# Expert 0's first two weight splits and two small copies on VectorE, and four loads in another order ahead of the constants

## The chip, the cores and the metric

The kernel runs on one core of a Trainium2 chip. The metric is device time in microseconds (us) of one execution; lower is better. The time before is the median of three runs. The profile and its trace are of one more execution, taken by the hardware profiler, and all times of instructions below are counted from the start of that execution's span.

## The reference

Three layers follow each other. The first is a gated linear attention (an mLSTM) over 768 steps for 2 batches of 8 heads of width 40; its output becomes 1536 rows of 320. The second is a mixture of 8 experts with a noisy router that picks two per row. The third is a dense layer with h·cos(h) between two products.

```python
for t in range(S):                                  # attention
    m_new = np.maximum(f_gate[:, :, t] + m, i_gate[:, :, t])
    f_stab = np.exp(f_gate[:, :, t] + m - m_new)
    i_stab = np.exp(i_gate[:, :, t] - m_new)
    C = f_stab[:, :, None, None] * C + i_stab[:, :, None, None] * np.einsum('bhd,bhe->bhde', vt, kt)
    n = f_stab[:, :, None] * n + i_stab[:, :, None] * kt
    y[:, :, t] = sigmoid(o_gate) * (C @ q) / np.maximum(np.abs(n @ q), 1.0)
...
noisy_logits = x @ w_gate + np.log1p(np.exp(x @ w_noise)) * noise        # experts
top2 = np.argpartition(-noisy_logits, 2, axis=1)[:, :2]
out[mask] += top2_w[mask, k, None] * (np.maximum(x[mask] @ w1[e], 0.0) @ w2[e])
...
h = x @ w_in; return (h * np.cos(h)) @ w_out                              # dense layer
```

## The kernel before, in words

**Attention.** The 768 steps of each batch are cut into 6 chunks of 128, so there are 12 chunks, numbered 0 to 11; chunk n is one call of `att_step(n)`. The gates of all chunks lie in one small tile (`g_all`, 16 rows); VectorE scans them in pieces (`gates_a`, chunks 0, 1, 2 to 3, 4 to 5). From chunk 2 on, the scanned gates are written to memory (`gd`, line 102) and read back spread over 128 partitions (`gb`, `load_gb`, line 175). `load_qk(n)` (lines 167, 168) fetches queries and keys into one of three buffers, `load_kv` and `load_o` the values and output gates. All of these go through the queue of SyncE (SP), which issues in the order of the program; an issue that waits holds everything behind it. `late_consts` (lines 370 to 372) fetches three constants over the same queue: `cc` (masks and ramps), `wc` (router weights) and `nz` (router noise). At the end of chunk 0 VectorE makes the mask `tri` from `cc` (line 891), ahead of its state update (line 293) and the scans of chunks 4 and 5 (line 90).

In a chunk, ScalarE makes the decay weights from `gb` (`mk_w`, line 209), GpSimd masks them (line 210), VectorE multiplies them into the scores (`mk_p`, line 256), TensorE makes scores (`mm_s`, line 247), outputs (`mm_out`, lines 306 and 310) and the state (`mm_state`, line 266, which reads `kb`, made by GpSimd at line 229). `mk_decay` (line 277) decays the state on GpSimd, `mk_q` (line 237) scales the queries on GpSimd or VectorE. `mk_y` makes the output rows `xt` on VectorE (line 327), a small copy of 64 columns follows (line 329, GpSimd in every chunk), and SP writes the rows to memory (`xd`, line 330). `rt_a` turns them on TensorE (line 342), `rt_b` multiplies by the router weights (line 351).

**Experts.** Beside chunks 8 to 11, batch 0 is routed: `router_d` on VectorE ends in the row numbers `idxe` (line 511), GpSimd gathers rows by them (`gather`, line 542, tile `xgt`), and `prep_slot` turns the gathered rows on TensorE (line 551). Weights come in by `load_w` over SP (`wraw`, line 528). `split(k)` takes piece k of them apart into two parts: ScalarE copies one (`wh`, line 580), and a subtraction makes the rest (`wl`, line 582), on GpSimd or VectorE by the rule at line 581. `expert_step` multiplies (`mm1` at line 589, `mm2` at lines 594 to 598). Experts 0 and 1 have first a group for batch 0 alone, which begins during chunk 10; split 0 is asked for after chunk 8 and split 1 after chunk 9. After chunk 11 the six other experts run, then the dense layer (`moe2_step`).

**Order.** Nothing reorders the program: each engine runs its instructions in the order in which the Python code emits them (`at`, `pre`, `mid` and `fill` say after which chunk a step is emitted), and semaphores keep the engines apart. Each DMA of SP also waits for the landing of the eighth DMA before it on that queue.

Of the kernel before, what the change touches and what calls it, by code (L numbers as in the profile page):

```python
# [22 lines left out]
DM = H * D  # L23
# [9 lines left out]
KW = 384  # L33
# [7 lines left out]
def tile_mlstm_moe_moe2(ctx, tc, qk, kv, og, gi, gf, wcat, noise, wm1, wm2, cst, out):  # L41
    nc = tc.nc
    V, A, G, T, Y = nc.vector, nc.scalar, nc.gpsimd, nc.tensor, nc.sync
# [79 lines left out]
    def gates_c(c0, c1):  # L123
        pv = PT[c0]
        V.tensor_copy(tok[:, c0:c1, :], pv[:, :, 0:16])
        if c0 < 2:
            V.tensor_copy(tokG[:, c0:c1, :], pv[:, :, 64:80])
        A.activation(kdec[:, c0:c1, :], pv[:, :, 32:48], AF.Exp)
# [23 lines left out]
    def load_o(i):  # L152
        t = OT[i] = mp.tile([128, 2, KO], FT, name="ogt", tag="wl" if i % 2 else "wh", bufs=4)
        Y.dma_start(t, og[:, 2 * i:2 * i + 2, :])
# [6 lines left out]
    def load_qk(n):  # L161
        if n >= 2 * NC:
            return
        b, c = divmod(n, NC)
        d = L[n]
        t = d["qk"] = QKS[n % NB]
        Y.dma_start(t[0:D, 0:3], qk[b, c, 0])
        Y.dma_start(t[64:64 + D, 1:4], qk[b, c, 1])

    def load_gb(n):  # L170
        if n >= 2 * NC:
            return
        b, c = divmod(n, NC)
        t = L[n]["gb"] = ap_.tile([128, H, C], FT, name="gb", bufs=3)
        Y.dma_start(t, bass.AP(tensor=GD.tensor, offset=GD.offset + (c * 16 + b * H) * C,
                               ap=[[0, 128], [C, H], [1, C]]))

    def load_kv(n):
        if n >= 2 * NC:
            return  # L180
        b, c = divmod(n, NC)
        d = L[n]
        t = ap_.tile([128, KO + H * (D + 1)], FT, name="kv", bufs=NB)
        Y.dma_start(t, kv[b, c])
        d["k"] = t[:, 0:KO].rearrange("p (h d) -> p h d", d=D)
        d["v"] = t[:, KO:].rearrange("p (h d) -> p h d", d=D + 1)
# [26 lines left out]
    def mk_e(n):  # L213
        if n >= 2 * NC:
            return
        b, c = divmod(n, NC)
        d = L[n]
        if c:
            e = d["ge"] = ap_.tile([128, NH, C], FT, name="get", bufs=2)
            for s in range(2):  # L220
                r = slice(64 * s, 64 * s + 64)
                if n >= 2:
                    A.activation(e[r], d["gb"][r, s:H:2, :], AF.Exp)
                else:
                    for u in range(2):
                        A.activation(e[r, 2 * u:2 * u + 2, :], d["pg"][u][r, s:4:2, :], AF.Exp)
        if c < NC - 1:
            kb = d["kb"] = KBS[n % 2]
            G.tensor_tensor(out=kb[:, :, 0:D], in0=d["k"],
                            in1=kdec[:, c, b * H:b * H + H][:, :, None].to_broadcast([128, H, D]), op=OP.mult)  # L230
# [19 lines left out]
    def mk_p(n):  # L250
        if n >= 2 * NC:
            return
        d = L[n]
        d["p"] = ap_.tile([128, H, C], FT, name="ppt", bufs=2)
        for u in range(2):
            V.tensor_tensor(out=d["p"][:, 4 * u:4 * u + 4, :],
                            in0=d["ps", u].rearrange("p (h t) -> p h t", t=C),
                            in1=d["w"][:, 4 * u:4 * u + 4, :], op=OP.mult)
# [56 lines left out]
    def mk_y(n):  # L315
        b, c = divmod(n, NC)
        d = L[n]
        pv = d["po"][:, :H * 41].rearrange("p (h e) -> p h e", e=41)
        den = ap_.tile([128, H, 1], FT, name="den", bufs=2)
        o = OT[n // 2][:, n % 2].rearrange("p (h d) -> p h d", d=D)  # L320
        A.activation(den, pv[:, :, D:D + 1], AF.Abs)
        V.tensor_scalar(den, den, 1.0, None, op0=OP.max)
        V.reciprocal(den, den)
        V.scalar_tensor_tensor(out=o, in0=o, scalar=1.0, in1=den.to_broadcast([128, H, D]),
                               op0=OP.add, op1=OP.mult)
        x = d["x"] = mp.tile([128, KW], FT, name="xt", bufs=3)
        V.scalar_tensor_tensor(out=x[:, :DM].rearrange("p (h e) -> p h e", e=D), in0=pv[:, :, 0:D], scalar=0.5,
                               in1=o, op0=OP.mult, op1=OP.mult)
        G.tensor_copy(x[:, DM:KW], x[:, 256:DM])
        Y.dma_start(XD[b * S + c * C:b * S + (c + 1) * C, :], x)  # L330


# [36 lines left out]
    def late_consts():  # L369
        Y.dma_start(cc_, cst[:, 128:469])  # L370
        Y.dma_start(wc, wcat)
        Y.dma_start(nz, noise)
# [158 lines left out]
    groups = [(e, T2, 2 * e) for e in (0, 1)]  # L531
# [36 lines left out]
        prep_x(d["xg"][i], groups[g][1][i], d["xh"], d["xl"], 128 * i, ps_)  # L568

    SP = {}  # L570
    POOL_SPLIT = (1, 7, 9, 11, 65, 67, 75)

    def split(k):
        g, f = divmod(k, 8)
        if g >= NG:
            return
        raw = WB[groups[g][0]]
        wh = mp.tile([128, FW], FR, name="wh", tag="wh", bufs=4)
        wl = mp.tile([128, FW], FR, name="wl", tag="wl", bufs=4)
        A.activation(wh, raw[:, f, :], AF.Copy)  # L580
        eng = V if len(groups[g][1]) == 2 and (k % 2 and k not in POOL_SPLIT or k in (12, 14)) else G
        eng.tensor_tensor(out=wl, in0=raw[:, f, :], in1=wh.bitcast(FT), op=OP.subtract)  # L582
        SP[k] = (wh, wl)

# [241 lines left out]
    gates_a(2, 4)  # L826
    gates_c(1, 2)
    mk_e(0)
    late_consts()
    load_gb(2)  # L830
    mk_p(0)
    mm_g(1)
    mk_w(1)
# [3 lines left out]
    gates_b(2, 4)  # L837

    def loads(n):
        load_qk(n + 3)  # L840
        if n > 2 or n == 0:
            load_gb(n + 3)
        load_kv(n + 2)
        if n < 5:
            load_o(n + 1)
        if n == 2:
            load_gb(4)
            load_gb(5)

    def att_step(n):  # L850
        if n == 0:
            loads(0)
# [27 lines left out]
        if n == 1:  # L880
            gates_a(4, NC)
        loads(n + 1)
        if n == 2 * NC - 1:
            mk_y(n)
        for f, a in fill.pop(n, []):
            f(*a)
        if n < 2 * NC - 1:
            mk_y(n)
# [36 lines left out]
    put(8, router_b1, 0, 1)  # L925
    put(8, router_s)
    put(8, split, 0)
    put(9, split, 1)
    mid[9] = [(router_c, (0,))]
    fill[9] = [(router_d, (0,)), (gather, (0, 0)), (gather, (0, 1))]  # L930
# [38 lines left out]
    for g in range(2, NG - 1):  # L969
        n = len(groups[g + 1][1])  # L970
# [21 lines left out]
    for f in range(12):  # L992
        k = 18 + (15 * f) // 4
# [36 lines left out]
    with tc.If(over > 0):  # L1030
# [9 lines left out]
        for b in range(B):  # L1040
            with tc.For_i(0, NC, 1) as it:
                x = mp.tile([128, KW], FT, name="xt", bufs=3)
# [10 lines left out]
                for e in range(E):  # L1053
                    acc = psA()
                    for f in range(8):
# [3 lines left out]
                        for k in range(3):  # L1059
                            n = 64 if k == 2 else 128  # L1060
# [98 lines left out]
```

## Time and profile before

| what | us |
|---|---|
| median of 3 runs | 523.4 (523.13 to 523.64) |
| profiled execution, its own time | 525.03 |
| its span | 523.3 |
| TensorE matmul busy | 490.2 (94%) |
| VectorE / ScalarE / GpSimd busy | 372.1 / 325.7 / 278.5 |

The span is nearly filled by TensorE, but matmuls are pipelined and a busy row of the profile also holds matmuls that run slowly, so the share alone does not say what a change is worth. What counts is where TensorE waits and for whom, and there the chain of waits helps: it goes back from the last instruction to whatever released each step. Its shares are TensorE 69%, VectorE 14%, DMA 7%, ScalarE 3%, GpSimd 2%; nearly all that is not TensorE lies in the first 135 us and around 300 to 330 us.

### The profile page before, as it was taken

How to read it: one execution, taken by the hardware profiler on the slowest of the kernel's cores; microseconds unless marked ns; L12 is line 12 of the kernel's file. 1: busy time of each engine (PE TensorE's matmuls, PEld its weight loads, DVE VectorE, ACT ScalarE, POOL GpSimd, SP SyncE). 2: the span in 40 equal slices, each digit the busy share in tenths (PEclk: the TensorE clock that was granted, in tenths of full speed). 3: DMA queues.
4: the chain of work that ended last, by engine and by line, in shares of the span. 5: the costliest groups of instructions: out<-in, count | busy, mean ns of one | idle time of the engine just before them, and what ended most of it. 6: DMA issues, size and time to landing. Idle time of an engine off the chain costs nothing.

```text
span 523.3 us, 9036 instructions
## 1 busy us (share of the span) xinstructions
PE 490.2 (94%) x3198; PEld 468.1 (89%) x3198; DVE 372.1 (71%) x791; ACT 325.7 (62%) x695; POOL 278.5 (53%) x246
## 2 busy tenths in 40 slices
PE   4799998999999999999999987999999999999994
PEld 3688887999899999999999976899999999999994
DVE  8774497678378777777775689688856665787772
ACT  3647867466465454545454655578787777777772
POOL 6445468665846867685857696274365347300000
PEclk9999999899999999999999999999999999999998
DMA  6789894695563828291929193030021003001001
GB/s 182 209 281 266 279 278 155 188 363 172 216 248 117 313 88 330 69 372 44 380 88 319 42 360 105 29 115 14 0 76 39 1 8 95 13 2 39 1 1 44
DMA packets 25909, 77.69 MB, mean 148 GB/s; under 512 B 3872, under 2 KB 11552, under 8 KB 25856
## 3 DMA queue, kind: packets, MB, share of 16 engines
q1 hardware_dynamic: 22752, 67.50, 37.2%
q0 software_dynamic: 3104, 9.54, 6.1%
q8 instruction: 27, 0.44, 0.3%
q14 instruction: 26, 0.21, 0.1%
HBM read 67.41 MB, written 9.62 MB: 147 GB/s over the span
## 4 chain that ended last, share of the span: by engine, by line
PE 69%; DVE 14%; DMA 7%; issue 4%; ACT 3%; POOL 2%; SPq 0%; DVEq 0%; POOLq 0%; ACTq 0%
PE pS L589 31%; PE pA L598 9%; PE pA L595 9%; PE pA L594 9%; DMA gb<-gd 2%; DMA xgt<-xd,idx 2%; PE pM L551 2%; PE pS L310 2%; PE pA L247 1%; PE pM L351 1%; PE pA L607 1%; PE pA L606 1%; POOL wl L582 1%; DVE xt L674 1%; DVE c_t L713 1%
## 5 line engine op out<-in xcount | busy, mean ns | idle before, releaser
L582 POOL TENSOR_TENSOR wl<-wraw,wh 128x704 fp32r<-128x704 f32 x69 | 122.9, 1787 | 59.9 <-ACT wh L580 56.3
L644 DVE SCALAR_TENSOR_TENSOR hb<-pS,hb 128x384 fp32r<-128x384 f32 (+2 forms) x128 | 45.9, 390 | 46.4 <-ACT hb L641 45.8
L580 ACT ACTIVATE wh<-wraw 128x704 fp32r<-128x704 f32 x80 | 62.8, 785 | 14.6 <-PE pA L606 8.2
L589 PE MATMUL pS<-xh,wh 128*128 128x448 f32 (+1 forms) x240 | 69.5, 344 | 0.4 <-ACT xh L553 0.4
L589 PE MATMUL pS<-xh,wl 128*128 128x448 f32 (+1 forms) x240 | 66.3, 330 | 0.9 <-POOL wl L582 0.9
L589 PE MATMUL pS<-xh,w 128*128 128x384 f32 x288 | 66.4, 339 | 0.5 <-DVE m_t L754 0.5
L594 PE MATMUL pA<-wh,hb 128*128 128x320 f32 x208 | 62.2, 309 | 0.0
L595 PE MATMUL pA<-wl,hb 128*128 128x320 f32 x208 | 62.2, 309 | 0.0
L739 ACT ACTIVATE m_t<-pS,magic 128x384 f32<-128x384 f32 x64 | 37.1, 579 | 30.4 <-PE pS L589 29.3
L641 ACT ACTIVATE hb<-pS 128x448 fp32r<-128x448 f32 (+1 forms) x80 | 37.6, 471 | 26.9 <-PE pS L589 20.0
L589 PEld LDWEIGHTS pS<-xh,w 128*128 128x128 f32 x288 | 50.0, 188 | 1.2 <-DVE m_t L754 1.1
L598 PE MATMUL pA<-wh,hb 128*128 128x320 f32 x208 | 44.3, 313 | 4.0 <-DVE hb L644 4.0
L754 DVE SCALAR_TENSOR_TENSOR m_t<-m_t,pS 128x384 f32<-128x384 f32 x64 | 35.4, 553 | 15.4 <-ACT m_t L753 15.1
L589 PEld LDWEIGHTS pS<-xh,wl 128*128 128x128 f32 x240 | 43.1, 190 | 3.3 <-POOL wl L582 1.1
L740 DVE TENSOR_SCALAR m_t<-m_t 128x384 f32<-128x384 f32 x64 | 23.3, 365 | 28.8 <-ACT m_t L739 28.6
L589 PEld LDWEIGHTS pS<-xh,wh 128*128 128x128 f32 x240 | 40.9, 190 | 1.4 <-ACT xh L553 0.6
L760 POOL TENSOR_TENSOR wl<-m_t,wh 128x384 fp32r<-128x384 f32 x25 | 25.4, 1017 | 31.0 <-ACT wh L758 21.7
L589 PE MATMUL pS<-xl,wh 128*128 128x448 f32 (+1 forms) x160 | 39.6, 329 | 0.0
L594 PEld LDWEIGHTS pA<-wh,hb 128*128 128x128 f32 x208 | 38.6, 186 | 0.6
L595 PEld LDWEIGHTS pA<-wl,hb 128*128 128x128 f32 x208 | 38.7, 186 | 0.6
L598 PEld LDWEIGHTS pA<-wh,hb 128*128 128x128 f32 x208 | 33.0, 186 | 6.0 <-DVE hb L644 5.9
L542 POOL DMA_INDIRECT xgt<-xd,idx x28 | 34.0, 1215 | 7.8 <-issue 3.4
(203 smaller groups left out, 1251.0 us busy)
## 6 DMA issues: line engine op xcount, KB each, us to landing
wraw<-wm SPq DMA_DIRECT2D x36, 704.0 KB
raw<-wm SPq DMA_DIRECT2D x16, 704.0 KB
qk<-qk SPq DMA_DIRECT2D x24, 240.0 KB
gb<-gd SPq DMA_DIRECT2D x10, 512.0 KB
kv<-kv SPq DMA_DIRECT2D x12, 324.0 KB
yd<-yt SPq DMA_DIRECT2D x22, 160.0 KB
wraw<-wm SPq DMA_DIRECT2D x8, 352.0 KB
xd<-xt SPq DMA_DIRECT2D x12, 192.0 KB
```

The lines of the kernel that those rows point to most:

```text
L542: G.indirect_dma_start(out=t[:n, :], out_offset=None, in_=XD[0:S, :] if g < 2 else XD[:, :], in_offset=bass.IndirectOffsetOnAxis(ap=(idxe ...
L580: A.activation(wh, raw[:, f, :], AF.Copy)
L582: eng.tensor_tensor(out=wl, in0=raw[:, f, :], in1=wh.bitcast(FT), op=OP.subtract)
L589: T.matmul(p[:, :n], w[:, 128 * k:128 * k + 128], x[:, m, :], start=(i == 0), stop=(i == 7))
L594: T.matmul(a[:n, :DM], hh[:, s], wh[:, KW:], start=first, stop=False)
L595: T.matmul(a[:n, :DM], hh[:, s], wl[:, KW:], start=False, stop=False)
L598: T.matmul(a[:n, :DM], hl[:, s], wh[:, KW:], start=False, stop=last)
L641: A.activation(hh[:, :n], p[:, :n], AF.Relu)
L644: V.scalar_tensor_tensor(out=hb[:, o:o + z - a], in0=p[:, a:z], scalar=0.0, in1=hh[:, a:z].bitcast(FT), op0=OP.max, op1=OP.subtract)
L739: A.activation(t, m["p"], AF.Identity, bias=magic, scale=0.5 / PI)
L754: V.scalar_tensor_tensor(out=s, in0=s, scalar=1.0, in1=m["p"], op0=OP.subtract, op1=OP.mult)
L760: eng.tensor_tensor(out=m["hl"], in0=m["t"], in1=m["hh"].bitcast(FT), op=OP.subtract)
```

## The change

There are three edits. The loads of chunk 2's gates and chunk 3's queries are emitted ahead of the three constants, and chunk 3's queries are no longer asked for in `loads(0)`. Splits 0 and 1 of expert 0 have their subtraction on VectorE in place of GpSimd. The small copy of chunks 9 and 10 is made by VectorE in place of GpSimd.

```diff
-        G.tensor_copy(x[:, DM:KW], x[:, 256:DM])
+        (V if n in (9, 10) else G).tensor_copy(x[:, DM:KW], x[:, 256:DM])
...
-    POOL_SPLIT = (1, 7, 9, 11, 65, 67, 75)
+    POOL_SPLIT = (7, 9, 11, 65, 67, 75)
...
-        eng = V if len(groups[g][1]) == 2 and (k % 2 and k not in POOL_SPLIT or k in (12, 14)) else G
+        eng = V if len(groups[g][1]) == 2 and (k % 2 and k not in POOL_SPLIT or k in (0, 12, 14)) else G
...
     mk_e(0)
+    load_gb(2)
+    load_qk(3)
     late_consts()
-    load_gb(2)
     mk_p(0)
...
     def loads(n):
-        load_qk(n + 3)
+        if n:
+            load_qk(n + 3)
```

On the queue of SP, right after the write of the scanned gates of chunks 2 and 3 (`gd`), this stands in the program (`+` now, `-` before; `gb` is chunk 2's gates where it has a sign and chunk 3's where it has none, `qk_88` chunk 3's queries):

```order
 L102 DMA gd<-g_all 16x4x128
+L175 DMA gb<-gd 128x1024
+L167 DMA qk_88<-qk 40x1536
+L168 DMA qk_88<-qk 40x1536
 L370 DMA cc<-cst 128x341
 L371 DMA wc<-wcat 128x48
 L372 DMA nz<-noise 128x96
-L175 DMA gb<-gd 128x1024
-L167 DMA qk_88<-qk 40x1536
-L168 DMA qk_88<-qk 40x1536
 L175 DMA gb<-gd 128x1024
 L184 DMA kv<-kv 128x648
```

The three loads have moved past the three constants; all else keeps its place.

On VectorE, at the end of chunk 8 and the start of chunk 9 (`r_rb` ends the router's step of chunk 8, `st_101` is the state update of chunk 9, `ppt` the scores for chunk 10):

```order
 L471 TENSOR_TENSOR r_so<-r_so,cc 128x8
 L472 TENSOR_TENSOR r_rb<-r_so,cc 128x8
+L582 TENSOR_TENSOR wl<-wraw,wh 128x704
 L293 TENSOR_TENSOR st_101<-pS,st_101 40x4x41 x2
 L256 TENSOR_TENSOR ppt<-pA,wt 128x512 x2
```

Split 0 now stands ahead of the state update, the scores and, further on, `router_d`.

On GpSimd, from the end of chunk 8 to chunk 10 (`kb_95` and `st_99` belong to chunk 10, the two gathers fetch expert 0's rows):

```order
 L210 AFFINE_SELECT wt<-wt 128x512 x2
-L582 TENSOR_TENSOR wl<-wraw,wh 128x704
 L229 TENSOR_TENSOR kb_95<-kv,kdec 128x8x40
 L277 TENSOR_TENSOR st_99<-st_101,get 40x4x41 x2
 L542 DMA xgt<-xd,idxe 128x384
 L542 DMA xgt<-xd,idxe 112x384
-L329 COPY xt<-xt 128x64
 L210 AFFINE_SELECT wt<-wt 128x512 x2
-L582 TENSOR_TENSOR wl<-wraw,wh 128x704
 L237 TENSOR_TENSOR qtt<-qk_93,get 128x512
```

Split 0 is gone from ahead of `kb` and the gathers; the copy of chunk 9 and split 1 are gone from behind them.

## Rows read from the trace of the kernel before

**Rows 1.** Chain of waits, 10 to 62 us: start, us, what
```profile
28.43 0.96 DVE g_all L96 x2
...
29.41 4.29 DMA gd<-g_all
...
33.76 5.75 DMA gb<-gd
```

**Rows 2.** Timeline of TensorE, 28 to 133 us; brackets: idle before, releaser
```profile
44.40 0.94 PE L351 MATMUL pM<-wc,xTt 128*128 128x128 f32 x6 [0.91 <-ACT xTt L344]
...
85.83 0.96 PE L266 MATMUL pS<-kv,kb 128*104 128x82 f32 x8 [1.05 <-POOL kb L229]
...
90.60 0.33 PE L342 MATMUL pM<-ident,xt 128*128 128x128 f32 x1 [0.92 <-POOL xt L329]
```

**Rows 3.** Timeline of all engines, 0 to 45 us
```profile
22.20 0.22 DVE L891 CAST tri<-cc 128x128 bf16<-128x128 f32 x1
...
24.76 0.67 PE L247 MATMUL pA<-qk 128*128 128x256 f32 x2 [2.02 <-DMA qk<-qk]
24.83 0.69 DVE L256 TENSOR_TENSOR ppt<-pA,wt 128x512 f32<-128x512 f32 x1 [0.47 <-POOL wt L210]
```

**Rows 4.** Chain of waits, 60 to 135 us
```profile
86.68 0.17 DVE idxe L511
...
87.80 0.32 POOL xgt L542
...
89.33 2.98 DMA xgt<-xd,idxe
...
94.48 2.39 PE pS L589 x16
```

**Rows 5.** Timeline of SP, 13 to 32 us
```profile
14.13 0.34 SPq L102 DMA_DIRECT2D gd<-g_all  x1
...
17.36 0.33 SPq L175 DMA_DIRECT2D gb<-gd  x1
...
18.15 0.33 SPq L168 DMA_DIRECT2D qk<-qk  x1
```

**Rows 6.** Windows: length; busy PE, PEld, DVE, ACT, POOL; granted clock; DMA share; GB/s
```profile
17.00:18.00 1.00, 0.84 (x9) 0.68 (x7) 0.24 (x2) 0.99 (x5) 0.77 (x2) 1.00 0.05 11
...
25.00:26.00 1.00, 1.00 (x9) 0.95 (x9) 1.00 (x2) 0.27 (x1) 0.00 (x0) 1.00 1.03 405
```

**Rows 7.** Timeline of GpSimd, 70 to 115 us
```profile
83.42 1.68 POOL L582 TENSOR_TENSOR wl<-wraw,wh 128x704 fp32r<-128x704 f32 x1
...
85.73 1.45 POOL L277 TENSOR_TENSOR st<-st,get 40x164 f32<-40x164 f32 x2
```

**Rows 8.** Groups by line and shape: busy us, mean ns of one, idle before
```profile
L582 DVE TENSOR_TENSOR wl<-wraw,wh 128x704 fp32r<-128x704 f32 x11 | 11.8, 1073 | 1.5 <-ACT wh L580 1.0 <-issue 0.4
...
L675 DVE COPY xt<-xt 128x64 f32<-128x64 f32 x12 | 3.7, 312 | 0.4
```

**Rows 9.** Timeline of VectorE, 70 to 115 us
```profile
88.01 0.49 DVE L327 SCALAR_TENSOR_TENSOR xt<-pS,ogt 128x320 f32<-128x320 f32 x1
...
92.29 0.42 DVE L554 TENSOR_TENSOR xl<-pA,xh 128x256 fp32r<-128x256 f32 x1 [3.71 <-ACT xh L553]
```

**Rows 10.** Timeline of SP, 76 to 112 us
```profile
90.58 0.34 SPq L330 DMA_DIRECT2D xd<-xt  x1
90.96 1.46 SPq L528 DMA_DIRECT2D wraw<-wm  x3
...
99.35 2.85 SPq L900 DMA_DIRECT2D yd<-cc  x3
```

**Rows 11.** The two gathers (tile `xgt`) of 98 to 102 us: issue to landing
```profile
DMA to landing us min/median/max: 3.6/4.6/5.6
```

**Rows 12.** Chain of waits, whole span, its beginning
```profile
1.28 1.91 DMA g_all<-gi
```

**Rows 13.** Windows of 1 us, columns as in group 6
```profile
93.00:94.00 1.00, 1.00 (x6) 1.00 (x6) 0.33 (x2) 0.45 (x1) 1.00 (x2) 0.50 0.75 200
```

## The prediction

> **What bounds the kernel now.** I read the chain of waits first, over two stretches, and then the timelines of the engines that it names. Behind 135 us TensorE follows TensorE nearly all the way, so whatever the change does must happen before that, in the attention and the start of the experts; what the chain loses there it loses for good, since TensorE has little idle time left in which to catch up.
>
> In the first stretch the chain runs through memory, not through an engine [rows 1]: VectorE ends the scans of chunks 4 and 5 at 29.39, their write `gd` takes 4.29 us to land, the read-back `gb` of chunk 4 another 5.75, so ScalarE can start on it at 39.5. TensorE stands idle 0.91 us for ScalarE at 44.40 [rows 2]. The `gd` write is small (16 rows of 256 numbers); that it takes 4.29 us says that it queues behind the loads issued before it. TensorE's largest single wait is earlier, 2.02 us at 24.76 for chunk 3's queries and keys [rows 3].
>
> In the second stretch the chain is VectorE up to the row numbers `idxe`, ready at 86.85, then GpSimd's first gather at 87.80, the second at 89.33, its landing 2.98 us later at 92.31, and only then TensorE [rows 4]. TensorE also waits 1.05 us for `kb` at 85.83 and 0.92 us for the copy of chunk 9 at 90.60 [rows 2], both for GpSimd. But these two waits lie ahead of 92.31, where TensorE stops in any case. They are idle time off the path.
>
> **The loads.** The first edit looks aimed at the wait at 24.76, and I do not see it help. The read of chunk 2's gates is issued at 17.36 [rows 5], not because three constants hold SP (three issues of some 0.34 us are 1 us of the 3.2 since 14.13) but because it reads what `gd`, issued at 14.13, has still to write. It stands ahead of chunk 3's queries before and after the change, so the queries go out by 18.15 as now, and land when they land now. Gain: 0, unless `gd` itself lands sooner (rival 2).
>
> What it costs is the constants' place. Now they move while the memory queues have nothing else: from 17 to 18 us the DMA share is down to 0.05, at 11 GB/s [rows 6]. Afterwards they go out behind the queries, into a stretch with a share of 1.03 at 405 GB/s [rows 6]. By their shapes they are 128 rows of 341, 48 and 96 numbers, 248 kB; at 405 GB/s that is 0.61 us. Everything behind them on SP's queue (chunk 3's gates, the next values, chunk 4's queries, in the end the `gd` write of 29.41) moves back by that much, because the chain's 4.29 us is a queue. Bounds: 0, if the constants fit into gaps; 1.2, at half that rate, since their rows are short. I take **+0.6** for ScalarE's start at 39.5, and so for TensorE at 44.40.
>
> There is a second cost. VectorE makes `tri` from `cc` at 22.20 [rows 3] and will have to wait for `cc`. Chunk 3's queries land at 24.76 by TensorE's release, `cc` behind them at about 25.2 (175 kB at the same rate). That stalls VectorE 3.0 us, with the state update, the scores and the scans of chunks 4 and 5 queued behind; 0.47 us of idle time on the way [rows 3] goes into it, so the scans end at 31.9 and not at 29.39. Does that add? From there the `gd` write needs 3.2 us, if I take what the earlier one needed until it released SP (14.13 to 17.36, rows 5), or 35.1; by the queue alone it lands at 33.70 + 0.6 = 34.3. The two are close, so I count the queue and put the other 0.8 in the range. The further waits on SP (each DMA waits for the eighth before it, and those land later now) delay loads that have a queue ahead of them anyway: 0, and up to 0.5 if that queue runs dry.
>
> **Split 0 on VectorE.** GpSimd gives up 1.68 us ahead of `kb` and the gathers [rows 7]; VectorE takes on one subtraction of 1.07 us mean [rows 8] ahead of `idxe`, which moves from 86.85 to 87.92. Now GpSimd is what the first gather waits for: its decay step ends at 87.18 [rows 7], and the gather starts 0.62 behind that. With the split gone GpSimd is early and VectorE late: the gather starts 0.1 to 0.6 us behind 87.92, at 88.0 to 88.5, which is 0.2 to 0.7 later than now. I take **+0.4**. The lower bound is -0.1: VectorE's steps there may run quicker once GpSimd does no split beside them. `kb` is ready 1.6 us earlier and TensorE's wait of 1.05 goes; but the next step, `mm_out` of chunk 10, needs VectorE's scores and queries, which come later by the 1.07, so TensorE waits there instead: 0.
>
> The Trainium skill (SBUF — State Buffer, section "Who interferes with whom") says that a VectorE instruction with two SBUF inputs and a GpSimd instruction that reads SBUF exclude each other for the whole instruction. Split 0 on VectorE stands beside `kb` on GpSimd, so by that rule `idxe` would slip by one more instruction of GpSimd, and the sum would be about 0.7 higher. The mean of 1.07 us in [rows 8] already holds subtractions beside a busy GpSimd, and nothing further is counted.
>
> **Split 1 and the two copies on VectorE.** 1.07 and twice 0.31 us [rows 8]; behind chunk 9's `xt` VectorE idles 3.71 us until 92.29 [rows 9], which covers 1.38; chunk 10's copy takes 0.31 ahead of a split that TensorE needs only a step later. The wait of 0.92 at 90.60 goes [rows 2]; TensorE comes to the gathered rows sooner and waits there longer: 0. But the copy also triggers something. SP writes chunk 9's rows when the copy is made: now at 90.58, with three weight loads behind from 90.96 [rows 10]. VectorE ends `xt` at 88.50 [rows 9], later 89.57; with 0.31 for the copy the write goes out at 89.9 and the loads from 90.3, 0.7 us earlier, and their data meets that of the second gather, which starts at 89.33 + 0.4 = 89.7. What such a meeting costs is shown one step later: beside the three `yd` writes issued from 99.35 [rows 10] the gathers need 3.6 and 5.6 us [rows 11], against 2.98. Bounds: 0 and +2.6. The loads come behind the gather's start here, and ahead of it there, so I take a value nearer the lower end, **+0.7**.
>
> The Trainium skill (DMA: Bandwidth & Descriptors, "Queues, rings and completion order") has each DMA engine take turns between its queues, a packet at a time. By that a gather beside one busy queue would need about twice its own transfer time; the 5.6 us of [rows 11] agree in kind. The sum stays.
>
> **Sum.** 0.6 + 0.4 + 0.7 = +1.7. The profiled execution, 525.03 with a span of 523.3, would become 526.7 with a span of 525.0. The median of 523.4 is 1.6 below that execution's own time; with the same difference, **525.1**. All lower bounds together give 523.3, all upper ones (1.2, 0.8, 0.5, 0.7, 2.6) 529.2, which I do not expect at once.
>
> **Rivals.** (1) *The bills are covered.* The constants slip through gaps of the queue, or the loads miss the gather; then one or two of the three terms stand, +0.4 to +1.0: 523.8 to 524.4. For it: the loads follow the gather's start. Against it: the `gd` write's 4.29 us, and the 5.6 us.
>
> (2) *Faster: `gd` lands sooner.* Place: SP's issue at 17.36, which waits 3.23 us for the write of 14.13 [rows 5]; a read of the gates at the program's start is back in 1.91 us [rows 12]. If the constants' transfers are what slows that write, then with them gone it lands up to 1.3 us sooner, chunk 2's gates and chunk 3's queries follow, and TensorE resumes at 23.5 in place of 24.76. Where the constants then fill the gap that this opens, the chain keeps the 1.3 at 44.40; with the gather at its -0.1 and no meeting that is -1.4: 522.0. Where they still cost their 0.6 it is -0.8: 522.6. It decides from the point where the gain at 17.36 passes the constants' bill. Against it: the loads issued ahead of `gd` would hold it just the same.
>
> (3) *TensorE's clock.* Here the granted clock was 0.50 in the us from 93 [rows 13], so 1.2 of 2.4 GHz, after TensorE had waited for the copy and the gathers, and 16 matmuls took 2.39 us [rows 4], of which about half would be saved at full clock. If the altered waits keep the clock up, that is -1.2 and the sum comes to +0.5: 523.9. If they stretch it, +1.2: 526.3. The waits do not get shorter in all, so I expect neither.
>
> (4) *All bills high*: the full 2.6 for the meeting and the scans' 0.8 too: 527.8.
>
> **Chances.** The forecast 0.44 (its own range 524.5 to 526.3, by the terms' bounds and the clock stretched); (1), with (3) and the clock kept, 0.31; (2) 0.17; (4) 0.08. A measurement of this kernel can tell 0.2%, or 1.05 us, from no change. Forecast and (4) are slower: 0.52. (2) is faster where it keeps the whole 1.3, 0.14, and the same where the constants' bill goes off, 0.03; with (1) the same has 0.34. The range of 8 in 10 leaves out (4) and what lies beyond (2): 522.0 to 526.8.
>
> **What would show it.** In the profile after, `tri` should start near 25, the issue of chunk 2's gates still stand at about 17.3, TensorE resume near 24.7, and the idle time at 44.40 stay, 0.6 us later. The first gather should start at 88.0 to 88.5 (plus that 0.6), the second one's landing need over 3.3 us, and TensorE's waits for `kb` and the copy be gone. I am wrong if TensorE resumes well before 24.7, if the first gather comes before 87.8, or if the second still lands within 3.0 us.

## The result and the profile after

| what | before | after |
|---|---|---|
| median, us | 523.26 (522.86 to 523.64, 4 runs) | 529.13 (527.91 to 530.2, 4 runs) |
| ratio after / before | | 1.0103 [1.0075, 1.013] |
| first profiled execution: own time, span | 525.03, 523.3 | 527.91, 526.2 |
| second profiled execution: own time, span | 522.66, 520.9 | 530.63, 528.9 |

The change makes the kernel 5.9 us slower; the forecast was +1.7 (525.1, with 522.0 to 526.8 as the range). By the ratio the 5.9 is 3.9 to 6.8. The two traces that come with the result differ by only 2.9 us, because the first profile of before is an execution above its median and the one of after is the lowest of its four. So each kernel was profiled once more among the experiments below. Here is TensorE's timeline in the second profile of before (start us, us, what; brackets: idle before, releaser):

```profile
42.36 0.94 PE L351 MATMUL pM<-wc,xTt 128*128 128x128 f32 x6 [0.29 <-ACT xTt L344]
...
82.45 0.91 PE L351 MATMUL pS<-wc,xTt 128*128 128x128 f32 x6
...
89.18 0.33 PE L342 MATMUL pM<-ident,xt 128*128 128x128 f32 x1 [0.91 <-POOL xt L329]
89.74 0.55 PE L551 MATMUL pA<-ident,xgt 128*128 128x128 f32 x3 [0.23 <-DMA xgt<-xd,idxe]
90.86 0.51 PE L551 MATMUL pA<-ident,xgt 112*128 112x112 f32 x3 [0.57 <-DMA xgt<-xd,idxe]
...
100.14 0.83 PE L351 MATMUL pM<-wc,xTt 128*128 128x128 f32 x6
```

The same timeline in the first profile of after:

```profile
43.78 0.94 PE L351 MATMUL pM<-wc,xTt 128*128 128x128 f32 x6 [1.51 <-ACT xTt L344]
...
83.95 0.91 PE L351 MATMUL pS<-wc,xTt 128*128 128x128 f32 x6
85.05 0.93 PE L266 MATMUL pS<-kv,kb 128*104 128x82 f32 x8 [0.19 <-POOL kb L229]
87.01 0.42 PE L306 MATMUL pS<-st,qtt 128*128 128x82 f32 x2 [1.03 <-DVE r_hi L509]
...
93.40 0.90 PE L551 MATMUL pA<-ident,xgt 128*128 128x128 f32 x3 [3.18 <-DMA xgt<-xd,idxe]
95.97 0.82 PE L551 MATMUL pA<-ident,xgt 112*128 112x112 f32 x3 [1.67 <-DMA xgt<-xd,idxe]
...
106.08 0.83 PE L351 MATMUL pM<-wc,xTt 128*128 128x128 f32 x6
```

Read the two against each other. At the router step of chunk 2 after is 1.42 behind (43.78 and 42.36), and still 1.50 behind at 82.45 and 83.95. Then come the gathers: at the second L551 it is 5.11 behind, so 3.6 are lost there. At the router step of chunk 10 it is 5.94 behind, and the spans differ by 5.3. Two places make nearly the whole difference between these two executions. In the first profile of before the first place can't be seen: its router step of chunk 2 stands at 44.40 [rows 2], 2.0 later than in the second profile of the same code. So the 1.4 of the first place is not yet the price of the change there; a table over all traces, further down, gives that.

The waits that the prediction spoke of went as it said: the 1.05 us for `kb` [rows 2] is down to 0.19, the 0.92 for chunk 9's copy is gone, and 1.03 us for VectorE's steps came in their place. What grew is the wait for the gathered rows: 0.23 and 0.57 us in the second profile of before, 3.18 and 1.67 now.

The chain of waits of after, same execution, names both places:

```profile
16.91 6.65 DMA cc<-cst
23.59 0.23 DVE tri L893
...
30.12 2.31 DMA gd<-g_all
32.50 6.40 DMA gb<-gd
...
89.81 6.12 DMA xgt<-xd,idxe
```

The second gather takes 6.12 us to land, where it took 2.98 [rows 4]. What stands beside it is on SP's queue (after, timeline of SP):

```profile
89.01 0.34 SPq L330 DMA_DIRECT2D xd<-xt  x1
89.40 1.40 SPq L528 DMA_DIRECT2D wraw<-wm  x3
```

In before the three weight loads went out at 90.96 [rows 10], 1.63 us behind the second gather's issue at 89.33. Now they go out 0.41 ahead of it (89.40 and 89.81). The stretches of TensorE and of the memory queues in after say the same (stretch, its length, busy us of each engine, granted clock, DMA share, GB/s):

```profile
90.00:92.00 2.00, 0.22 (x2) 0.00 (x0) 0.00 (x0) 1.74 (x4) 1.94 (x4) 1.00 0.84 224
92.00:94.00 2.00, 0.60 (x3) 0.50 (x3) 0.00 (x0) 0.00 (x0) 1.25 (x2) 0.67 0.99 368
94.00:96.00 2.00, 0.33 (x3) 0.03 (x1) 0.72 (x2) 0.49 (x1) 0.00 (x0) 0.50 0.64 213
96.00:98.00 2.00, 2.00 (x10) 2.00 (x11) 0.66 (x2) 0.45 (x1) 0.00 (x0) 0.50 0.00 0
98.00:100.00 2.00, 2.00 (x13) 2.00 (x13) 1.91 (x5) 1.22 (x3) 0.79 (x1) 0.63 0.00 0
```

For six us TensorE does next to nothing (0.22, 0.60 and 0.33 us busy) while the queues are busy (shares of 0.84, 0.99 and 0.64). The gather lands at 95.93, when the queues run empty: the small gather is done no sooner than the 1 MB of weights. The granted clock, the last but two figure, falls after TensorE has stood idle from 90.2; it is half (1.2 GHz) for some 6.8 us, from 92.7 to 99.5, and the last 3.5 of these TensorE works through.

On VectorE and GpSimd the split moved as planned (after, timelines of both):

```profile
83.47 0.88 DVE L582 TENSOR_TENSOR wl<-wraw,wh 128x704 fp32r<-128x704 f32 x1
83.50 1.43 POOL L229 TENSOR_TENSOR kb<-kv,kdec 128x320 f32<-128x320 f32 x1
...
86.19 0.68 DVE L237 TENSOR_TENSOR qtt<-qk,get 128x512 f32<-128x512 f32 x1
...
87.23 0.17 DVE L511 TENSOR_SCALAR idxe<-idx 128x4 uint32<-128x4 f32 x1
...
88.26 0.49 DVE L327 SCALAR_TENSOR_TENSOR xt<-pS,ogt 128x320 f32<-128x320 f32 x1
88.79 0.20 DVE L329 COPY xt<-xt 128x64 f32<-128x64 f32 x1
```

And VectorE in the first profile of before, two of the same steps and the row numbers:

```profile
85.30 1.02 DVE L237 TENSOR_TENSOR qtt<-qk,get 128x512 f32<-128x512 f32 x1
...
86.68 0.17 DVE L511 TENSOR_SCALAR idxe<-idx 128x4 uint32<-128x4 f32 x1
86.76 0.45 DVE L322 TENSOR_SCALAR den<-den 128x8 f32<-128x8 f32 x1
```

The row numbers come 0.55 later in after (86.68 and 87.23), chunk 9's `xt` only 0.25 later (88.01 [rows 9] and 88.26), though a split of 0.88 us stands ahead of both. VectorE gets part of it back: its scaling of the queries takes 0.68 in place of 1.02.

### The profile page after: what moved, and what is told of

Read it like the earlier page. It is cut to its first block, busy times and chain, and to the rows that moved or that the text cites. A ratio compares the mean times of both kernels' runs of the same rounds, so it can differ in the third digit from the quotient of the medians.

```text
span 526.2 us, 9031 instructions
## 1 busy us (share of the span) xinstructions
PE 490.6 (93%) x3198; PEld 469.2 (89%) x3198; DVE 372.2 (71%) x795; ACT 325.4 (62%) x695; POOL 274.9 (52%) x242
## 4 chain that ended last, share of the span: by engine, by line
PE 72%; DVE 14%; DMA 4%; ACT 4%; issue 3%; POOL 1%; SPq 0%; DVEq 0%; ACTq 0%; POOLq 0%
PE pS L589 33%; PE pA L598 10%; PE pA L595 10%; PE pA L594 10%; PE pM L551 2%; PE pA L607 1%; PE pA L606 1%; PE pS L310 1%; DMA cc<-cst 1%; PE pM L351 1%; DMA gb<-gd 1%; DMA xgt<-xd,idxe 1%; ACT wt L209 1%; PE pA L247 1%; DVE xt L674 1%
## 5 line engine op out<-in xcount | busy, mean ns | idle before, releaser
L582 POOL TENSOR_TENSOR wl<-wraw,wh 128x704 fp32r<-128x704 f32 x67 | 119.6, 1792 | 65.6 <-ACT wh L580 61.0
```

## The experiments

All differences are against runs of before made on the same chip; "over before" is the difference of the medians. The ratio with its 95% interval is not the quotient of the medians and differs from it by up to 0.2%, which is 1 us; a difference of a few tenths is therefore not settled by its digits. The theories at the outset: A, chunk 9's copy on VectorE sends the weight loads into the gathers; B, the splits hold up the row numbers; C, the constants' new place.

### One edit at a time

**Chunk 9's copy alone.** Before, with this edit only:

```diff
-        G.tensor_copy(x[:, DM:KW], x[:, 256:DM])
+        (V if n in (9,) else G).tensor_copy(x[:, DM:KW], x[:, 256:DM])
```

> The kernel before with one edit: chunk 9's small copy on VectorE. Theory A (the meeting): SP writes chunk 9's rows and asks for the three weight loads as soon as the copy is made, near 88.8 us in place of 90.58, so their data meets both gathers, which start at 87.8 and 89.3 as before; the second gather needs 5 to 6 us to land in place of 3.0, and the run is 3 to 6 us slower than the kernel before. Theory B (VectorE's splits hold up the row numbers) and theory C (the constants' new place) expect no change, within 0.5 us.

Measured: 527.13 us (526.58 to 528.77, 6 runs), 3.7 over before, ratio 1.0088 [1.0067, 1.011], so 3.5 to 5.8 us. The chain of waits and TensorE's timeline:

```profile
88.20 5.44 DMA xgt<-xd,idxe
...
93.68 0.82 PE L551 MATMUL pA<-ident,xgt 112*128 112x112 f32 x3 [2.72 <-DMA xgt<-xd,idxe]
```

One 64-column copy (0.47 us on VectorE in this trace, 0.20 in after) makes most of the loss. The weight loads go out at 88.30, 0.10 behind the second gather, and it needs 5.44 us to land.

**Splits 0 and 1 alone.**

```diff
-    POOL_SPLIT = (1, 7, 9, 11, 65, 67, 75)
+    POOL_SPLIT = (7, 9, 11, 65, 67, 75)
...
-        eng = V if len(groups[g][1]) == 2 and (k % 2 and k not in POOL_SPLIT or k in (12, 14)) else G
+        eng = V if len(groups[g][1]) == 2 and (k % 2 and k not in POOL_SPLIT or k in (0, 12, 14)) else G
```

> The kernel before with one edit: splits 0 and 1 on VectorE. Theory A: the first gather starts at about 88.3 in place of 87.8, the copy of chunk 9 stays behind the gathers on GpSimd, the weight loads stay behind 90.5 and the second gather still lands in about 3.0 us; 0 to 0.7 us slower than before. Theory B: most of the 5.9 us of the change, 3 us or more. Theory C: no change.

Measured: 523.88 (12 runs), 0.5 over before, 1.0026 [1.0004, 1.0048]. The interval is 0.2 to 2.5 us, so theory B, which wanted 3 or more, falls.

**The load order alone**, the first edit as the change has it.

> The kernel before with one edit: chunk 2's gates and chunk 3's queries asked for ahead of the constants. Theory A: the gates go out at 15.7 in place of 17.4, TensorE resumes about 1 us earlier at 24, and this is given back by 57 us, where it waits for chunk 7's queries; total -0.6 to +0.3 us. Theory C: 2 us or more slower. Theory B: no change.

Measured: 524.38 (12 runs), 1.0 over before, 1.0022 [1.0008, 1.0035]: more than theory A's -0.6 to +0.3 and less than theory C's 2. By the medians the three parts sum to 3.7 + 0.5 + 1.0 = 5.2 of the 5.9; by the ratios they sum to 7.1, against 5.4 for the change. The next run asks whether they add.

**The change without its load order.**

> The changed kernel with the load order of before: splits 0 and 1 and both copies on VectorE, nothing else. By the sum of the single edits (3.7 + 0.5 over before) 527.3 to 528.3, about 1.0 below the changed kernel. If the load order works only together with the rest, or not at all: 528.6 to 529.4.

Measured: 527.45 (6 runs), 3.9 over before, 1.0059 [1.0036, 1.0083]; the sum of the two parts was 4.2.

### Is it the copy, or what it sets off?

**The change with expert 0's weight loads earlier**, so that none is left behind chunk 9's rows:

```diff
-        put((6, 7, 8, 8, 8, 9, 9, 9)[i], load_w, 0, i, 1)
+        put((6, 7, 7, 7, 7, 8, 8, 8)[i], load_w, 0, i, 1)
```

> The changed kernel with one more edit: the last three of expert 0's eight weight loads are asked for after chunk 8 and three others after chunk 7, so that none is asked for after chunk 9. Theory A: with no weight data on the memory queues the gathers land in 3.0 to 3.5 us although chunk 9's rows are still written early; the time falls to 522.5 to 524.5. Theories B and C: it stays at 528 to 530.

Measured: 525.85 (524.87 to 527.41, 6 runs), 2.5 over before, 1.0053 [1.0034, 1.0073]: 3.4 of the 5.9 are gone, with the copy still on VectorE, but it stays above the 522.5 to 524.5 that I had expected. Its chain of waits:

```profile
89.91 3.66 DMA xgt<-xd,idxe
```

The second gather is still 0.7 slower than in before; beside it now runs only the 192 kB write of chunk 9's rows, issued at 89.10.

**The earlier weight loads in the kernel before** show that they are no gain of their own.

> Before, with the weight loads of expert 0 after chunks 6, 7, 7, 7, 7, 8, 8, 8 in place of 6, 7, 8, 8, 8, 9, 9, 9, and nothing else. Theory A takes this shift for free by itself (the loads had no part in a wait of before): 523.0 to 523.8, so that the 3.3 us it saved in the changed kernel are those of the meeting. Rival E (the shift is a gain of its own, since before already pays for weight loads beside the second gather's end): 521.0 to 522.5.

Measured: 523.39 (12 runs), 1.0009 [0.9986, 1.0031]. The shift alone is no gain that can be measured, so the 3.4 us are the meeting's.

**The change with chunk 9's copy back on GpSimd**:

```diff
-        (V if n in (9, 10) else G).tensor_copy(x[:, DM:KW], x[:, 256:DM])
+        (V if n in (10,) else G).tensor_copy(x[:, DM:KW], x[:, 256:DM])
```

> The changed kernel with one thing undone: chunk 9's small copy is back on GpSimd (chunk 10's stays on VectorE). Theory A (the 5.9 us come mostly from the copy of chunk 9, which sends the weight loads into the gathers): the copy alone cost 3.7 over before, the splits alone 0.5, the load order alone 1.0, so this kernel keeps 1.5 of the 5.9 and stands at 524.4 to 525.4; SP's write of chunk 9's rows is back behind 90, the second gather lands within 3.2 us. Rival B (the three edits need each other, for example the splits delay the gathers into the weight loads whatever the copy does): 526.5 or more, with the second gather over 4 us. Rival C (chunk 9's copy on GpSimd now waits behind both gathers, and TensorE waits over 1 us for it): 525.5 to 526.5.

Measured: 524.72 (523.23 to 526.02, 12 runs), 1.1 over before, 1.0025 [1.0011, 1.0038]; theory A had 524.4 to 525.4. Rival B falls; rival C wanted 525.5 or more and over 1 us of waiting for the copy. TensorE waits 0.98 us for it again, no more than in before, and the 1.1 that are left are no more than the splits and the load order cost alone (0.5 and 1.0).

**A meeting without the copy.** Before, with the last three weight loads asked for one chunk earlier:

```diff
-        put((6, 7, 8, 8, 8, 9, 9, 9)[i], load_w, 0, i, 1)
+        put((6, 7, 8, 8, 8, 8, 8, 8)[i], load_w, 0, i, 1)
```

> Before, with the copies and splits as they were, but the last three weight loads of expert 0 asked for after chunk 8 in place of chunk 9, so six of 352 KB each are issued from about 82.7 and are still moving when the gathers go out at 87.8 and 89.3. Theory A (what costs is weight data beside the gathers, and the copy only set it off): the gathers take 1 to 3 us longer to land though no copy has moved, 524.4 to 526.5. Rival B (it is the copy or VectorE's order, not the loads): 523.2 to 523.9.

Measured: 524.31 (12 runs), 0.8 over before by the medians, 1.0008 [0.9993, 1.0024]: below theory A's range, and not to be told from zero. TensorE's timeline shows why it is small:

```profile
92.10 1.46 PE L551 MATMUL pA<-ident,xgt 128*128 128x128 f32 x6 [2.03 <-DMA xgt<-xd,idxe]
```

Here the loads are issued ahead of both gathers, and they run out while the gathers wait. The first gather, issued at 86.92, lands 5.2 us later (3.4 in the second profile of before, 86.38 to 89.74), but then the second is there too: both are done 5.2 us behind the first one's issue, against 4.5 (86.38 to 90.86). In this trace the gathers do wait longer without the copy having moved. That the price hangs on how much of the loads is still to come is my reading of the traces; this run's time does not show it.

### What the load order costs

**The constants' transfer by itself.** Before, with the three constants loaded a second time, into tiles that nothing reads, behind chunk 3's queries:

```diff
...
+    def more_consts():
+        Y.dma_start(cc2, cst[:, 128:469])
+        Y.dma_start(wc2, wcat)
+        Y.dma_start(nz2, noise)
...
     def loads(n):
         load_qk(n + 3)
+        if n == 0:
+            more_consts()
```

> Before, with the load of the three constants (248 kB) issued a second time, into tiles that nothing reads, right behind chunk 3's queries, where the change puts the constants; the first copy stays where it was, so the mask on VectorE is not delayed and the gates' write and read keep their neighbours. Theory C (the 1.0 us of the load order is the constants' transfer in a stretch in which the memory queues are full): 524.0 to 524.8, with a TensorE wait for chunk 7's queries near 51 or a later start of ScalarE at 39.5. Rival F (the 1.0 us comes from the mask made later on VectorE, or from the gates sooner): 523.2 to 523.6.

Measured: 523.57 (12 runs), 1.0005 [0.999, 1.0021]. 248 kB more in that stretch cost nothing that can be measured. Theory C in this form falls.

**`cc` kept ahead**: the new order, but with the load of `cc` (now `late_consts(0)`) in its old place.

```diff
...
-    late_consts()
+    late_consts(0)
     load_gb(2)
+    load_qk(3)
+    late_consts(1)
...
     def loads(n):
-        load_qk(n + 3)
+        if n:
+            load_qk(n + 3)
```

> Before with the change's load order, but the first of the three constants, `cc`, stays ahead of chunk 2's gates; only `wc` and `nz` go behind chunk 3's queries. Theory F1 (the 1.0 us of the load order is the mask, which VectorE then makes later, 22.2 to 24.3 in the trace of the load order alone): mask back at about 22.2 and 523.1 to 523.8, no slower than before. Theory F2 (it is chunk 2's gates and chunk 3's queries going ahead, whatever the mask does): 524.1 to 524.8.

**The gates alone ahead** of the constants:

```diff
-    late_consts()
     load_gb(2)
+    late_consts()
```

> Before with one step of the load order alone: chunk 2's gates are asked for ahead of the three constants, chunk 3's queries stay behind them. Theory F1 (the mask made later is what costs): the mask is made at 23 or later here too, 524.0 to 524.8. Theory F2 (the queries' place): the queries stand behind the constants as before, 523.2 to 523.8.

Measured: 524.04 (12 runs), 1.0009 [0.9993, 1.0025], and 523.83 (12 runs), 1.0005 [0.9989, 1.0021]. In both traces the mask is made at 22.2, as in before; for the second I had expected it later. The first time lies between the ranges of F1 and F2 (523.8 and 524.1). Neither run can be told from before, nor, by its interval, from the 1.0 of the load order.

**A larger dose.** Before, with `cc` alone moved behind chunk 0's other loads:

```diff
+    def late_cc():
+        Y.dma_start(cc_, cst[:, 128:469])
+
     def late_consts():
-        Y.dma_start(cc_, cst[:, 128:469])
...
         if n < 5:
             load_o(n + 1)
+        if n == 0:
+            late_cc()
```

> Before with `cc` alone asked for later still, behind chunk 0's other loads (gates of chunk 3, values, output gates); `wc` and `nz`, chunk 2's gates and chunk 3's queries in the order of before. Theory F1 (the load order costs by the mask that VectorE makes later, with the scans of chunks 4 and 5 behind it): the mask comes at 24 to 26, the scans' end moves by the same 2 to 4 us from about 28 to 29, and the time goes up by more than in the load order alone, 524.5 to 526.5. Theory F2 (the place of the gates and queries): 523.0 to 523.9.

Measured: 528.23 (524.87 to 529.98, 9 runs), 4.9 over before, 1.008 [1.0055, 1.0105], more than I had expected. VectorE and TensorE in its timeline:

```profile
26.70 0.23 DVE L895 CAST tri<-cc 128x128 bf16<-128x128 f32 x1 [4.43 <-DMA cc<-cst]
...
31.55 0.73 DVE L96 TENSOR_TENSOR_SCAN g_all<-g_r,g_all 16x128 f32<-16x128 f32 x2
...
45.75 1.65 PE L351 MATMUL pM<-wc,xTt 128*128 128x128 f32 x6 [2.93 <-ACT xTt L344]
```

A mask made 4.5 later moves the scans' end to 32.28 and the router step of chunk 2 to 45.75, 3.4 behind the second profile of before and 1.35 behind the first. So a mask that comes this late is on the path, through the scans of chunks 4 and 5. Here too half clock follows the wait, from 44.6 to 51.4, and the next router step comes 9.3 us later (6.6 there), so this execution loses another 2.7.

**The new order with all constants at the program's start**, and the same with the three edits of the next section (a version without the meeting).

```diff
     load_qk(2)
+    late_consts()
...
-    late_consts()
     load_gb(2)
+    load_qk(3)
...
-        load_qk(n + 3)
+        if n:
+            load_qk(n + 3)
```

> The change's load order alone, with the three constants asked for at the program's start, behind chunk 2's queries, where SP is idle from 6.4 to 14.1. Theory F1: the mask is back at 22.2, so the 1.0 us goes, 522.8 to 523.8. Theory F2 (gates and queries ahead cost by themselves): 524.1 to 524.8. If the first write of the gates now queues behind the constants and lands later than 17.4: 524 or more, with SP's issue of chunk 2's gates behind 17.4.

> The form of the change that the runs so far point to: split 0 on GpSimd behind the gathers, chunk 9's copy on VectorE, no weight load behind chunk 8, and the constants at the program's start. By the runs so far 522.5 to 523.5, that is, no worse than before and perhaps 0.1% better; if the constants at the start hold up the gates: 523.8 or more.

Measured: 525.1 (522.29 to 529.48, 12 runs), 1.0032 [1.0008, 1.0056], and 524.8 (522.06 to 528.58, 12 runs), 1.0015 [0.9993, 1.0038]. The first is a miss for the mask theory: the mask is back at 22.2, and it is slower all the same. Its profiled execution (523.99) does not hold the loss, apart from chunk 2's gates, issued at 17.07 against 16.13 in the second profile of before. The second, slower than the 522.5 to 523.5 expected, has a trace (526.23) that shows a loss: TensorE waits 1.79 us for chunk 3's queries, behind gates issued at 17.21, and then runs at half clock from 25.1 to 31.9.

```profile
24.53 0.67 PE L247 MATMUL pA<-qk 128*128 128x256 f32 x2 [1.79 <-DMA qk<-qk]
...
32.90 0.94 PE L351 MATMUL pM<-wc,xTt 128*128 128x128 f32 x6
```

This router step, chunk 0's, stands at 28.50 and 29.84 in the two profiles of before. But the first of those waits 2.02 us at the same place and keeps its clock, so one trace does not say how often this happens; why constants at the start cost something, and why these runs spread over 7 us, stays open. For the load order itself, the mask fits: it comes late in the load order alone (1.0022) and in the larger dose (1.008), and the three runs with it at 22.2 and the constants not at the start (the second copy, `cc` ahead, gates ahead) come out at 1.0005 to 1.0009. Their intervals reach up to 1.0025, so they do not exclude another part. One is in the trace of the load order alone (527.0, the highest of its 12): TensorE waits 1.52 us at 53.08 for chunk 7's queries and then runs at half clock for some 3.4 us. The second profile of after has such a wait too (0.96), none of the others has; no run tests it by itself.

### A version without the meeting

Before, with split 0 on GpSimd but behind the gathers, chunk 9's copy on VectorE, and the earlier weight loads:

```diff
-        put((6, 7, 8, 8, 8, 9, 9, 9)[i], load_w, 0, i, 1)
+        put((6, 7, 7, 7, 7, 8, 8, 8)[i], load_w, 0, i, 1)
...
-    put(8, split, 0)
+    put(9, split, 0)
```

> Before, with the idea of the change in another form: split 0 stays on GpSimd but is emitted after chunk 9 (behind the gathers), chunk 9's copy is on VectorE, and the weight loads of expert 0 come after chunks 6, 7, 7, 7, 7, 8, 8, 8, so none is asked for behind chunk 9's rows. Load order and split 1 as before. Theory A: the wait for kb (1.05 us) and the one for chunk 9's copy (0.92) go, nothing new meets the gathers but the 192 kB write of chunk 9's rows: the first gather starts at about 87.8 as before, the second lands in 3.0 to 3.7 us, 522.4 to 523.6, no slower than before. Rival D (the early copy costs by itself, through the write of chunk 9's rows): 524.0 to 525.0.

Measured: 523.38 (522.11 to 524.94, 12 runs), 0.9994 [0.9976, 1.0011]. The early copy is harmless once no weights follow it, and taking the waits for `kb` and the copy away gains nothing that can be measured: TensorE waits for the gathers instead.

### Both kernels profiled again

> The kernel before, profiled once more. If the profiled execution of before was one of the slower ones in its first 60 us (its own time of 525.03 stands 1.6 over the median), a second one should show chunk 2's gates issued before 17.0, TensorE back before 24.4 and its router step of chunk 2 starting before 44.0 (in the first: 17.36, 24.76, 44.40); if these are the same in every execution, they come again within 0.2 us.

Measured: 522.66. Chunk 2's gates are issued at 16.13 (17.36 in the first), TensorE is back at 23.42 (24.76), the router step of chunk 2 stands at 42.36 (44.40). The same code, and 2.0 us apart by 45 us.

> The changed kernel, profiled once more, to be laid beside the second profile of before. In the first profile of after TensorE stood at half clock from 14.16 to 17.58, and VectorE came late to the mask for that reason as well as for `cc`. If the load order is what makes the front later, this one shows the mask waiting for `cc` and made between 23.3 and 24.4, the scans' end at 29.9 to 30.7 (28.88 in the second profile of before) and TensorE's router step of chunk 2 at 43.6 to 44.1 (42.36 there), whether or not the clock falls; the second gather lands over 5 us behind its issue, and the time is 527.5 to 530.5. If it was the clock alone, a profile without it shows the scans' end before 29.5 and the step before 43.2.

Measured: 530.63. Its timeline of VectorE, its chain, and its timeline of TensorE:

```profile
24.11 0.23 DVE L893 CAST tri<-cc 128x128 bf16<-128x128 f32 x1 [1.83 <-DMA cc<-cst]
...
29.69 0.73 DVE L96 TENSOR_TENSOR_SCAN g_all<-g_r,g_all 16x128 f32<-16x128 f32 x2
...
43.91 0.94 PE L351 MATMUL pM<-wc,xTt 128*128 128x128 f32 x6 [1.06 <-ACT xTt L344]
...
90.32 6.37 DMA xgt<-xd,idxe
...
97.35 1.51 PE L351 MATMUL pM<-wc,xTt 128*128 128x128 f32 x6
...
107.86 0.38 PE L351 MATMUL pM<-wc,xTt 128*128 128x128 f32 x2
```

The mask waits 1.83 us for `cc`, the scans end at 30.42 (28.88 in the second profile of before), and the router step of chunk 2 is 1.55 behind, without the early stretch of half clock that the first profile of after had (14.2 to 17.6). So the wait for `cc` comes from the load order. That the step then stands 1.55 later does not follow from two profiles: the second one of before is the earliest of all nineteen traces there. Laid side by side (two traces with other losses left out, the larger dose and the second one with the constants at the start):

| traces | mask made | router step of chunk 2 | router step of chunk 8 |
|---|---|---|---|
| 10 with the mask on time | 22.2 | 42.36 to 44.40, median 43.15 | 82.33 to 84.20, median 82.93 |
| 5 with the change's load order | 23.44 to 24.32 | 43.78 to 44.04, median 43.91 | 83.95 to 86.80, median 84.17 |
| 2 with the load order of before, half clock from 14.4 to 17.7 | 23.28 and 23.35 | 43.70 and 44.74 | 83.89 and 85.74 |

By the medians the late mask goes with 0.8 us at chunk 2 and 1.2 at chunk 8, in step with the 1.0 of the load order alone. In the last two a slow TensorE, not `cc`, made VectorE late at the mask, and the front is late as well.

In the second profile of after the second gather takes 6.37. The step from 97.35 to 107.86 takes 10.5 us, against 8.9 in the second profile of before (91.20 to 100.14), where the clock stays full: here it is half from 88.75 to 102.40, and that is another 1.6. It fell while TensorE was at work, 1.2 us behind the 1.03 us wait for VectorE.

## Why the prediction was wrong

The time, 529.13, lies outside the range of 522.0 to 526.8, and the step that failed is the price of the meeting.

**The meeting, the term that failed.** The sum had +0.7 for it; alone it measures +3.7 (3.5 to 5.8 by its interval), and in the traces the second gather's rows come 3.6 and 3.9 us later, counted from the router step of chunk 8. The mechanism was named with its trigger and its place. What went wrong is the step that dates the loads: "later 89.57; with 0.31 for the copy the write goes out at 89.9 and the loads from 90.3, 0.7 us earlier". They went out at 89.40, 1.56 earlier. I had passed the whole split, 1.07 us, on to `xt`. It took 0.88, VectorE's own steps ran faster once GpSimd had done with its part (`qtt` 1.02 to 0.68, `den` 0.45 to 0.16), and the copy took 0.20, not 0.31. By my dates the loads came 0.6 behind the second gather, and for that I took a value near the lower bound. In fact they came 0.4 ahead of it. The upper bound of 2.6 was too low as well: it came from gathers beside three writes of 560 kB in all [rows 11], and here stood 1 MB of loads; 6.12 - 2.98 is 3.1. A gap of 1.6 us between two events, on which the whole term hung, was estimated with an error of 1 us, and then only one side of it was priced.

**The constants: size about right, path wrong.** The sum had +0.6 from the queue behind them; the load order measures +1.0 (0.4 to 1.8). The second copy of the constants finds no cost of the queue (-0.5 to +1.1 us by its interval). The path that I had worked out beside it (VectorE waits for `cc`, the scans end at 31.9) and counted as "the other 0.8" of the range is the one that the runs point to: the mask at 23.6 and 24.1, the scans' end at 30.1 and 30.4. Nor is the 4.29 us of the `gd` write the fixed queue on which the +0.6 was built: it took 2.31 in the first profile of after and 2.30 in the second of before.

**Split 0: the size right, the step by luck.** +0.4, measured +0.5 for both splits (0.2 to 2.5 by the interval); the first gather starts at 88.33, in the 88.0 to 88.5 foretold. But two errors cancel. I had `idxe` move by 1.07, the mean of subtractions of which one took 2.84 us; the split took 0.88, VectorE's scaling ran faster behind it, and `idxe` moved by 0.55. And I had the gather wait for GpSimd's decay step, so that only 0.4 of the 1.07 would reach it. In all nineteen traces the first gather starts 0.93 to 0.95 us behind the end of `idxe`, also in after, where GpSimd had been idle for 2.44 us: what `idxe` loses, the gather loses whole. That `kb`'s wait would turn into one for VectorE's scores and queries came out as written (1.03 us). By the Trainium skill (SBUF — State Buffer, "Who interferes with whom") split and `kb` exclude each other, and I had named another 0.7 us for `idxe` by that rule. The trace agrees with the lock, but the loser was GpSimd: the split, begun at 83.47, took its 0.88, and `kb`, begun at 83.50, went from 0.72 to 1.43.

**Split 1, copy waits: right.** They were off the path; the earlier copy was worth nothing that can be measured.

**Rival 2, `gd` sooner: in part so, without a gain.** In after the gates are issued at 15.74 and TensorE resumes at 23.66, well before 24.7, which I had named as a sign against me. But before does nearly the same in its second profile (16.13 and 23.42). Over the traces the gates go out at 15.74 to 16.67 with the change's load order (five, median 15.78) and at 16.06 to 17.59 with that of before (nine, median 16.65). So `gd` does land sooner, by some 0.9 us, but no run gains by it. The rows of the wait at 24.76 and of the 4.29 us write [rows 1, 3] were those of an execution whose front ran late; a gain was read into them that another execution of the same code doesn't have to give.

**Rival 3, the clock: it stretched.** I expected neither. The step behind the gathers takes 9.50 and 10.51 us in the two profiles of after and 9.37 and 8.94 in those of before. The first profile of before holds 3.4 us of half clock there (one of them in [rows 13]), the second none. From the router step of chunk 8 to that of chunk 10, the half clock included, the thirteen traces in which the second gather lands within 3.4 us take 17.67 to 18.56 us (median 18.5), the first and second profile of after 22.13 and 23.40. So of the 5.9 us some 3.6 to 4.9 are the gathers' wait with the half clock behind it, and about 1 the load order.

**Rival 4, all bills high** (527.8, a chance of 0.08), comes nearest to what happened. Its mechanism is the forecast's with the full price.

## What to carry to other kernels

An edit that frees a DMA's trigger earlier must be costed by what the queue holds behind that DMA, and with the distance to the latency-bound transfer beside it: here loads 1.6 us behind the gather were free, and loads 0.1 us behind it cost 3.7. Where a price jumps at such a distance, put the error of both dates against it before choosing an end of the range. And read a wait from several executions before building on it: one profiled execution can hold 2 us that the next does not, and that next one can be the earliest of all.

## What was not expected of the hardware

- The second gather (112 rows) took 2.9 to 3.0 us to land with the weight loads issued 1.6 us behind it, 3.2 to 3.7 beside one write of 192 kB issued 0.8 us ahead of it, 5.4 with 1 MB of loads issued 0.1 us behind it, and 6.1 to 6.4 with them 0.4 ahead. In the first profile of after it landed as the loads ran out.
- The clock fell to half for 6.8 and 13.7 us around the longer waits of after (6.8 also with the copy alone), for 3.4 and 0 us in the two profiles of before.
- VectorE's split and GpSimd's `kb`, begun 0.03 us apart, were slowed by very different amounts: the split not at all (0.88 us, as the second split beside a gather), `kb` to twice its time (0.72 to 1.43).
- A second load of 248 kB into a stretch with a DMA share of about 0.9 did not show in the time, while the runs in which VectorE waited 2.0 and 4.4 us for one of these constants were slower by 1.0 and 4.9.
